# Attention's additions over key chunks moved from GpSimd to VectorE, its copies spread to ScalarE, and the conversions of a later stage spaced evenly

## The chip, the core and the metric

The kernel runs on one core of a Trainium2 chip. A core has five engines with queues of their own, each of which works through its instructions in order: TensorE (PE in the rows, its weight loads PEld), VectorE (DVE), ScalarE (ACT), GpSimd (POOL) and SyncE (SP), which here issues nearly all DMA transfers (SPq). The metric is the device time of one execution in microseconds; the program is run several times and the median counts.

## What is computed

Three steps follow on each other, all in fp32 as the reference has them:

```python
scores = scale * np.matmul(q, k.transpose(0, 1, 3, 2))      # (4, 12, 448, 64) each
scores = cap * np.tanh(scores / cap)
attn = np.exp(scores - np.max(scores, axis=-1, keepdims=True))
attn = attn / (np.sum(attn, axis=-1, keepdims=True) + 1e-09)
x = np.matmul(attn, v)                # then to 1792 tokens x 768
...
logits = x @ phi                      # soft mixture: 8 experts x 4 slots
slot_input = softmax_over_tokens(logits).T @ x
h = np.maximum(slot_input[e] @ w1[e], 0.0); slot_out[e] = h @ w2[e]
x = softmax_over_slots(logits) @ slot_out
...
h = x @ w_in; g = s * np.maximum(h, 0.0)**2 + b; out = g @ w_out
```

`w_in` and `w_out` come in 64-bit words, and have to be made fp32 on the chip before TensorE can use them.

## The kernel before

Three stages run one after the other.

**Attention with the slot inputs.** The 48 heads are handled as 24 pairs of two heads. The 448 keys of a pair lie in four chunks j: three of 128 keys for both heads (tiles of 128x896), and one of 64 keys with the two heads stacked (128x448). For each chunk TensorE makes scores (`emit_qk`, L486, tile sp), ScalarE applies tanh (L494) and exp (L508) into a tile e, and TensorE multiplies with v into one PSUM tile for the whole pair (`emit_av`, L529, and L534 for the last chunk; tile av, of which there is only one). When a pair ends, a copy takes av to xu (L410 on VectorE, L408 on ScalarE), and only then may the next pair's first L529 run. Scores are made one pair ahead of their use, from q and k that TensorE transposes (L443) and that a copy puts into qs and ks.

The denominators need the sum of e over all keys. `emit_es` (L516) adds the three large chunks of a pair elementwise into a tile es, two additions of 128x896; `emit_esl` (L521) adds the last chunk, one half-wide addition per head. TensorE then sums over partitions with a matrix of ones (`emit_den`, L552, tile dn), once for two pairs (a quad, g). Reciprocals, the logits of the mixture (lg), the transposed and normalized x (xt, xq) follow once per quad, and per six pairs (a batch) a running softmax over tokens and three slot products (sl). The last of the 24 pairs has no additions for its last two chunks: `emit_den` takes them as further terms of the matmul.

**Slots.** slp, w1 (h1p, L946) and w2 (so, L967) of the eight experts. Their weights, 25 MB for w1 and 25 MB for w2, come by DMA; ten blocks of w1 and ten of w2 are loaded while attention runs, the last six w2 blocks into the room that the conversions below leave (`cend`, which waits for the last of them). Further blocks are loaded as attention's own tiles come free at its end.

**The last two products,** PE bound, with 32 loads' worth of weights. Twenty of the 32 blocks of 64-bit words are converted while attention runs, and written to scratch memory (scr): load (`cl`, L201), two bit operations on VectorE (`conv_a`, L214 and L217), a conversion of the low words on ScalarE (`conv_f`, L224), an addition (`conv_m`, L227, VectorE or GpSimd), and the store (`cst`, L334). Two load tiles (ring w) and three result tiles exist.

**What sets the order.** Nothing in attention is ordered by hand. `ListSchedule` gets every operation with the engines that can do it and a planned duration on each (`engs`), what it needs, its priority, the ring buffers that it takes and gives back, an earliest start (`after`) and a latency until users may start (`lat`, 0.2 unless given). It plays the program through with these numbers, always placing next on the engine that can start first, and writes the instructions out in that order. Each engine then runs its list in order; a wait at the head of a list holds up all that stands behind it. Where two engines can do an operation, the planned end decides, with a surcharge where one is given: GpSimd's additions have 2.3 and 1.2, VectorE's 1.3 and 0.68 with surcharges DES and DESL, and a copy on ScalarE has the surcharge HACT. The same code with other sizes exists a second time behind a flag for inputs out of range; it doesn't run here.

Of the kernel before, what the change touches and what calls it, by code (L numbers as in the profile page):

```python
# [28 lines left out]
ACT, DVE, POOL, PE, SP = "ACT", "DVE", "POOL", "PE", "SP"  # L29


class ListSchedule:

    def __init__(self, rings):
        self.bufs = rings
        self.ops = {}

    def add(self, name, engs, fn, need=(), prio=0.0, acq=(), rel=(), after=0.0, lat=0.2):

        self.ops[name] = dict(
            engs=engs, fn=fn, need=list(need), prio=prio, acq=acq, rel=rel, after=after, lat=lat
        )

    def run(self):
        end, free, freed, holds = {}, {}, {}, {}
        got = {r: [] for r in self.bufs}
        waits, after = {}, {}  # L50
        for name, o in self.ops.items():
            need = set(o["need"])
            waits[name] = len(need)
            for d in need:
                after.setdefault(d, []).append(name)
            for x in o["rel"]:
                holds[x] = holds.get(x, 0) + 1
        ready = [name for name, n in waits.items() if n == 0]
        while ready:
            best = {}  # L60
            for name in ready:
                o = self.ops[name]
                t = max([o["after"]] + [end[d] for d in o["need"]])
                for ring, _ in o["acq"]:
                    k = len(got[ring]) - self.bufs[ring]
                    if k >= 0:
                        t = max(t, freed.get((ring, got[ring][k]), 1e9))
                if t < 1e8:
                    _, t, eng, dur = min(
                        (max(t, free.get(e, 0.0)) + d + sum(x), max(t, free.get(e, 0.0)), e, d)  # L70
                        for e, d, *x in o["engs"]
                    )
# [7 lines left out]
            end[name] = free[eng] + o["lat"]  # L80
            for ring, owner in o["acq"]:
# [14 lines left out]
def kernel(  # L96
# [16 lines left out]
    nc = tc.nc  # L113
    B, H, S, D = q.shape
# [171 lines left out]
    def run(safe):  # L286
        W1N, W2N = (4, (4,)) if safe else (10, (4, 6))
        NV, NEB, NEL, NES, NXU, NXQ, NQK = 2, 4, 2, 2, 4, 3, 2
        PX, PA, DES, DESL, HACT = -0.32, 1.5, 4.98, 1.5, 0.96
        CV0, CVP, CVA, WA = 9.33, 6.53, 20.19, 30.39  # L290

        PT, PDEN, PLG, PLW, PXT, PXM, PSO, PSL = -2.67, 1.0, 2.0, 3.4, 3.33, 2.05, 0.25, 4.75
        wctx = ExitStack()
# [76 lines left out]
        ones = c1_p.tile([128, 128], F32, name="ones")  # L370
# [22 lines left out]
        KC = S // 128  # L393
# [4 lines left out]
        spt, et, est, xut = {}, {}, {}, {}  # L398
# [4 lines left out]
        def tp(name):  # L403
            return ps_t.tile([128, 512], F32, tag="tp", name=name)
# [137 lines left out]

        def emit_den(g, _):
            pst["den", g] = ps = tp("dn")
            for j in range(4):
                n, h = 2 * g + j // 2, j % 2
                parts = [(slice(0, 128), est[n][:, h])]
                if n == NP - 1:
                    rows = slice(KL * h, KL * h + KL)
                    parts += [(slice(0, 128), et[n, KC - 1][:, h]), (rows, et[n, KC][rows, 0])]  # L550
                for i, (rows, x) in enumerate(parts):
                    nc.tensor.matmul(  # L552
                        out=ps[32 * j:32 * j + 32, 0:S], lhsT=ones[rows, 0:32], rhs=x,
                        start=(i == 0), stop=(i == len(parts) - 1),
                    )

        def emit_row_c(which, g, e):
            dnt[which, g] = t = sb_p.tile([128, S], F32, tag="dn", name="dn")
# [160 lines left out]
        ))  # L719

        def op(name, engs, f, need=(), prio=0.0, acq=(), rel=(), **kw):
            sch.add(name, engs, lambda e: f(*name[1:], e), need, prio, acq, rel, **kw)

        def cp(dve=True, hact=HACT):
            return [(DVE, 0.62)] * dve + [(ACT, 0.53, hact)]

        LAT = 2.0
        op(("const",), [(SP, 0.1)], load_const, prio=3.0, lat=LAT, after=2.0)
        for n in range(NP):
            f = 2 * n  # L730
            for w in "qk":
                i = ("ld", w, n)
# [3 lines left out]
            i = ("ld", "v", n)  # L736
# [8 lines left out]
            for j in range(KC + 1):  # L745
                u, m = f + j * 2 / (KC + 1), 1 if j < KC else 0.5
# [9 lines left out]
                rel = [(ring, (n, j))]  # L756
                if 0 < j < (KC if n < NP - 1 else KC - 1):
                    op(
                        ("es", n, j), [(POOL, 2.3), (DVE, 1.3, DES)], emit_es,
                        [("exp", n, j), ("exp", n, 0) if j == 1 else ("es", n, j - 1)], u + 1,  # L760
                        [("es", n)] if j == 1 else [], rel + [("e", (n, 0))] * (j == 1),
                    )
                if j == KC and n < NP - 1:
                    for h in range(2):
                        op(
                            ("esl", n, h), [(POOL, 1.2), (DVE, 0.68, DESL)], emit_esl, [("exp", n, j), ("es", n, j - 1)],
                            u + 1, [], rel,
                        )
                op(
                    ("av", n, j), [(PE, 0.85)], emit_av, [("exp", n, j), i] + [("av", n, j - 1)] * (j > 0), u + PA,  # L770
# [4 lines left out]
        for g in range(NQ):  # L775
            bb, gq = divmod(g, NQUAD)
            u0, last = 4 * g + 4, g == NQ - 1
# [6 lines left out]
            op(("den", g), [(PE, 0.82)], emit_den, es, u0 + PDEN, [("tp", ("den", g))], rel)  # L784
            if last:
                for j in range(2):
                    sch.add(
# [558 lines left out]
```

## Time and profile before

| what | value |
|---|---|
| times of three runs | 663.97, 662.75, 657.78 us, median 662.75 |
| the profiled execution | 664.11 us, its span 662.3 us |
| TensorE busy | 607.6 us (92%) |
| VectorE busy | 369.0 us (56%) |
| ScalarE busy | 396.5 us (60%) |
| GpSimd busy | 199.6 us (30%) |
| first scores, last product of attention with v | 9.4 us, 293.7 us |
| slots' first product (slp) | 305.9 us |
| first large product of the last stage (L1197) | 382.9 us |

The page gives each engine's busy time over the whole span, and then the span in 40 slices; the stages have different limits, so the shares of the whole say little. The rows of the next section are from the chain of work that ended last, from sums over stretches, from single instructions in order of time, and from groups by tile. In a row an idle time before an instruction stands in brackets with what ended it. The granted clock of TensorE (PEclk) is 1.00 at 2.4 GHz and 0.50 at 1.2 GHz.

### The profile page before, as it was taken

Reading aid. Unit: us, or ns where it says so; the run is one execution under the profiler, and the core shown is the slowest. Engines: PE = TensorE matmul, PEld = TensorE weight load, DVE = VectorE, ACT = ScalarE, POOL = GpSimd, SP = SyncE. Lnnn points to the kernel's source line nnn. Section 1 sums busy time; section 2 is a strip of 40 time slices with the busy share of each in tenths; the row PEclk is TensorE's granted clock in tenths of the full one; section 3 lists DMA queues with packets and bytes.
Section 4 is the critical chain, followed back from the end, with each engine's and each line's share of the span. In section 5 each row is a group of like instructions: output and inputs, shape, how many; then the busy total and the mean of one; then the engine's idle time right before and its main releaser. Section 6 shows DMA issues by size and latency. Waiting matters only on the chain.

```text
span 662.3 us, 10246 instructions
## 1 busy us (share of the span) xinstructions
PE 607.6 (92%) x3994; PEld 361.7 (55%) x3994; DVE 369.0 (56%) x518; ACT 396.5 (60%) x566; POOL 199.6 (30%) x116
## 2 busy tenths in 40 slices
PE   6979989889899999987985689999999999999995
PEld 3323333333233333333652368888888888888784
DVE  2397877768974445335460158992467669611221
ACT  4884876677666775720000188886666666656683
POOL 1694647576755555500000153421000000000000
PEclk9998989899999999996997789999999999999998
DMA  8675998979978531239999997340587779200201
GB/s 153 176 239 164 322 283 276 310 240 294 293 242 254 193 70 29 78 126 345 405 402 405 397 367 254 133 140 1 177 310 255 247 250 328 102 1 1 95 1 53
DMA packets 110345, 139.27 MB, mean 210 GB/s; under 512 B 52432, under 2 KB 84944, under 8 KB 110288
## 3 DMA queue, kind: packets, MB, share of 16 engines
q1 hardware_dynamic: 109344, 138.43, 63.6%
q8 instruction: 33, 0.54, 0.3%
q10 hardware_dynamic: 944, 0.10, 0.1%
q14 instruction: 24, 0.20, 0.1%
HBM read 125.14 MB, written 13.37 MB: 209 GB/s over the span
## 4 chain that ended last, share of the span: by engine, by line
PE 74%; DMA 12%; DVE 9%; ACT 2%; issue 1%; POOL 1%; SPq 0%; DVEq 0%; ACTq 0%; POOLq 0%
PE y L1197 23%; PE y L1198 12%; PE sp L486 10%; PE av L529 8%; DMA w2c<-in_moe_w_dram 5%; PE tr L443 3%; DMA w<-in_moe_w_out_dram 3%; PE av L534 2%; DVE cm L217 2%; PE h1p L946 2%; PE dn L552 2%; DVE cm L214 2%; PE xt L612 2%; PE gp L1129 2%; DMA w<-in_moe_w_in_dram 2%; DMA w<-scr 2%
## 5 line engine op out<-in xcount | busy, mean ns | idle before, releaser
L494 ACT ACTIVATE e<-sp,tsc 128x896 f32<-128x896 f32 x96 | 87.2, 911 | 78.9 <-PE sp L486 77.5
L1197 PE MATMUL y<-wo,gh 128*128 128x512 f32 x336 | 127.0, 400 | 0.0
L1174 DVE TENSOR_TENSOR gl<-r,gh 128x512 fp32r<-128x512 f32 (+1 forms) x65 | 44.5, 685 | 102.3 <-ACT r L1159 102.2
L486 PE MATMUL sp<-qs,ks 64*128 64x448 f32 (+1 forms) x384 | 98.4, 592 | 0.0
L1198 PE MATMUL y<-wo,gh 128*128 128x256 f32 x336 | 94.4, 281 | 0.0
L508 ACT ACTIVATE e<-e,capt 128x896 f32<-128x896 f32 x96 | 89.7, 946 | 1.8
L529 PE MATMUL av<-e,vn 128*64 128x448 f32 x288 | 74.0, 591 | 5.5 <-DVE xu L410 5.5
L516 POOL TENSOR_TENSOR es<-e 128x896 f32<-128x896 f32 x24 | 51.1, 2129 | 88.4 <-ACT e L508 55.0
L1146 ACT ACTIVATE r<-gp 128x512 f32<-128x512 f32 (+1 forms) x65 | 35.0, 539 | 60.8 <-PE gp L1129 59.3
L1197 PEld LDWEIGHTS y<-wo,gh 128*128 128x128 f32 x336 | 63.2, 188 | 13.8 <-issue 1.6
L1197 PE MATMUL y<-wo,gl 128*128 128x512 f32 x168 | 66.7, 397 | 0.0
L1198 PEld LDWEIGHTS y<-wo,gh 128*128 128x128 f32 x336 | 63.1, 188 | 1.7
L268 DVE TENSOR_REDUCE rng<-w 128x1 f32<-128x768 f32 x64 | 56.9, 944 | 0.0
L217 DVE SCALAR_TENSOR_TENSOR cm<-w,cm 128x768 int32<-128x768 int32 x32 | 53.3, 1664 | 1.1
L486 PEld LDWEIGHTS sp<-qs,ks 64*128 64x128 f32 (+1 forms) x384 | 28.1, 178 | 44.4 <-issue 24.1
L521 POOL TENSOR_TENSOR es<-es,e 64x448 f32<-64x448 f32 x35 | 49.3, 1410 | 8.4 <-ACT e L508 6.2
L516 POOL TENSOR_TENSOR es<-es,e 128x896 f32<-128x896 f32 x23 | 50.7, 2206 | 3.7 <-ACT e L508 2.7
L1159 ACT ACTIVATE r<-r,bt,st 128x512 f32<-128x512 f32 (+1 forms) x65 | 49.1, 756 | 1.8
L1159 ACT ACTIVATE gh<-r,bt,st 128x512 fp32r<-128x512 f32 (+1 forms) x65 | 49.1, 757 | 1.6
L1198 PE MATMUL y<-wo,gl 128*128 128x256 f32 x168 | 47.1, 281 | 0.0
L1197 PE MATMUL y<-woe,gh 128*128 128x512 f32 x112 | 44.3, 418 | 0.0
L214 DVE TENSOR_SCALAR cm<-w 128x768 int32<-128x768 int32 x32 | 35.4, 1107 | 15.5 <-DMA w<-in_moe_w_out_dram 8.4
(152 smaller groups left out, 907.8 us busy)
## 6 DMA issues: line engine op xcount, KB each, us to landing
w<-in_moe_w_in_dram SPq DMA_DIRECT2D x32, 768.0 KB, 5.8
w<-in_moe_w_out_dram SPq DMA_DIRECT2D x32, 768.0 KB, 6.1
w1c<-in_moe_w_dram SPq DMA_DIRECT2D x24, 1024.0 KB, 9.5
w2c<-in_moe_w_dram SPq DMA_DIRECT2D x26, 768.0 KB, 12.7
scr<-cm SPq DMA_DIRECT2D x20, 384.0 KB, 5.1
w<-scr SPq DMA_DIRECT2D x20, 384.0 KB, 5.9
qn<-in_q_dram SPq DMA_DIRECT2D x24, 224.0 KB, 4.1
kn<-in_k_dram SPq DMA_DIRECT2D x24, 192.0 KB, 4.3
```

The lines of the kernel that those rows point to most:

```text
L214: nc.vector.tensor_scalar(out=m, in0=hi, scalar1=3, scalar2=0x3FFFFFF8, op0=ALU.logical_shift_left, op1=ALU.bitwise_and)
L217: nc.vector.scalar_tensor_tensor(out=m, in0=hi, scalar=-0x40000000, in1=m, op0=ALU.bitwise_and, op1=ALU.bitwise_or)
L268: nc.vector.tensor_reduce(out=rng[:, j, i:i + 1], in_=hi, axis=AX.X, op=o, apply_absolute_value=True)
L486: nc.tensor.matmul(out=sp[:, h, 0:S] if j < KC else sp[KL * h:KL * h + KL, 0, 0:S], lhsT=ks[n][rows, 128 * j:min(128 * j + 128, S)], rhs=q ...
L494: nc.scalar.activation(out=e, in_=spt.pop((n, j))[:, 0:m, 0:S], func=AF.Tanh, scale=tsc)
L508: nc.scalar.activation(out=e, in_=e, func=AF.Exp, scale=capt)
L516: eng.tensor_tensor(out=t, in0=et[n, 0] if j == 1 else t, in1=et[n, j], op=ALU.add)
L521: eng.tensor_tensor(out=t, in0=t, in1=et[n, KC][KL * h:KL * h + KL, 0], op=ALU.add)
L529: nc.tensor.matmul(out=out, lhsT=vt[n][:, KC * h + j, :], rhs=et[n, j][:, h], start=(j == 0), stop=False)
L1159: nc.scalar.activation(out=out, in_=in_, func=AF.Identity, scale=st, bias=bt)
L1197: nc.tensor.matmul(out=ya, lhsT=lhsT, rhs=w[:, 0:512], start=first, stop=last)
L1198: nc.tensor.matmul(out=yb, lhsT=lhsT, rhs=w[:, 512:768], start=False, stop=last and i0 == per - 1)
```

## The change

It edits numbers and rules of the planner, and one loop.

- es and esl may only go to VectorE, with planned durations 1.1 and 0.63; so may the conversion's addition. In the order printed from the program, GpSimd had 47 additions of 128x896, 35 of 64x448 and 7 of the conversion in attention; VectorE had 11 and 13. Now VectorE has all 47, 46 and 20. GpSimd keeps four small additions (`lall`).
- A new rule `port` lets operations marked with it not overlap in the plan between VectorE and GpSimd.
- The surcharge of a copy on ScalarE, HACT, falls from 0.96 to 0.1. VectorE had 84 of the 96 copies and ScalarE 12; now it is 50 and 46.
- Conversions: load i may start at 20.19 + 9.5 i of the plan (CVT) rather than all from 20.19 on, with a latency of 3.0 rather than 2.0; their priority rises (CVP).
- All operations but scores, tanh and exp get a planned latency of 0.6 (LATE).
- `emit_den` of the last quad takes its further terms term by term over the four groups of 32 columns, rather than group by group.

```diff
-    def add(self, name, engs, fn, need=(), prio=0.0, acq=(), rel=(), after=0.0, lat=0.2):
+    def add(self, name, engs, fn, need=(), prio=0.0, acq=(), rel=(), after=0.0, lat=0.2, port=()):
...
+        def start(o, e, t):
+            return max(t, free.get(e, 0.0), port[0] if e in o["port"] else 0.0)
...
-        PX, PA, DES, DESL, HACT = -0.32, 1.5, 4.98, 1.5, 0.96
-        CV0, CVP, CVA, WA = 9.33, 6.53, 20.19, 30.39
+        PX, PA, HACT = -0.32, 1.5, 0.1
+        CV0, CVP, CVA, CVT, WA = 9.33, 2.0, 20.19, 9.5, 30.39
+        LATE = 0.6
...
-                parts = [(slice(0, 128), est[n][:, h])]
+                parts.append([(slice(0, 128), est[n][:, h])])
...
-                for i, (rows, x) in enumerate(parts):
-                    nc.tensor.matmul(
...
+            for i in range(3):
+                for j in range(4):
+                    if i < len(parts[j]):
+                        rows, x = parts[j][i]
+                        nc.tensor.matmul(
...
+            kw = {"lat": LATE if name[0] not in ("qk", "tanh", "exp") else 0.2, **kw}
...
-                        ("es", n, j), [(POOL, 2.3), (DVE, 1.3, DES)], emit_es,
+                        ("es", n, j), [(DVE, 1.1)], emit_es,
...
-                            ("esl", n, h), [(POOL, 1.2), (DVE, 0.68, DESL)], emit_esl, [("exp", n, j), ("es", n, j - 1)],
+                            ("esl", n, h), [(DVE, 0.63)], emit_esl, [("exp", n, j), ("es", n, j - 1)],
...
-            op(("cl", i), [(SP, 2.19)], cv_load, [], pr - 6, [("w", i)], lat=LAT, after=CVA)
-            op(("ca", i), [(DVE, 2.0)], cv_a, [("cl", i)], pr, [("cm", i), ("ce", i)], [("w", i)])
+            op(("cl", i), [(SP, 2.19)], cv_load, [], pr - 6, [("w", i)], lat=3.0, after=CVA + CVT * i)
+            op(("ca", i), [(DVE, 1.55)], cv_a, [("cl", i)], pr, [("cm", i), ("ce", i)], [("w", i)], port=BOTH)
...
-            op(("cmul", i), [(DVE, 1.23), (POOL, 1.83)], cv_m, [("cf", i)], pr, [], [("ce", i)])
+            op(("cmul", i), [(DVE, 0.95)], cv_m, [("cf", i)], pr, [], [("ce", i)], port=BOTH)
```

The lines of the changed kernel stand 7 to 14 higher (L410 is L418, L521 is L529, L552 is L564). Three places show what the new numbers do to the order.

VectorE early in attention, at the end of the third pair, before: the third conversion (w_437) stands ahead of the copy of that pair (xu).

```order
L521 TENSOR_TENSOR es<-es,e 64x448
L214 TENSOR_SCALAR cm<-w_437 128x768
L217 SCALAR_TENSOR_TENSOR cm<-w_437,cm 128x768
L410 COPY xu<-av 128x448
L410 COPY qs<-tr 128x448
L410 COPY ks<-tr 128x448
L588 TENSOR_TENSOR lw<-rowt,rd 112x512
```

The same place now, from the copy xu of that pair on; the first conversion's addition is the row ahead of it.

```order
L234 ISA cm<-cm,ce 128x1536
L418 COPY xu<-av 128x448
L600 TENSOR_TENSOR lw<-rowt,rd 112x512
L524 TENSOR_TENSOR es<-e 128x896
L609 TENSOR_REDUCE lall<-lw 112x128
L524 TENSOR_TENSOR es<-es,e 128x896
L629 TENSOR_TENSOR xq<-xt,rd 112x4x128
L529 TENSOR_TENSOR es<-es,e 64x448 x2
L629 TENSOR_TENSOR xq<-xt,rd 112x4x128
L221 TENSOR_SCALAR cm<-w_432 128x768
L224 SCALAR_TENSOR_TENSOR cm<-w_432,cm 128x768
```

The additions of a pair now stand between the other work of VectorE, and the second conversion comes a whole pair's work after the copy.

TensorE at the last quad before: the sums dn of the last two pairs, between the last pair's products with v.

```order
L529 MATMUL av<-e,vn 64x448 x2
L552 MATMUL dn<-es,ones 32x448 x3
L552 MATMUL dn<-e,ones 32x448 x2
L552 MATMUL dn<-es,ones 32x448
L552 MATMUL dn<-e,ones 32x448 x2
L529 MATMUL av<-e,vn 64x448 x2
L565 MATMUL rowt<-ident,dn 112x128 x4
L534 MATMUL av<-e,vn 64x448 x2
```

And now:

```order
L537 MATMUL av<-e,vn 64x448 x2
L564 MATMUL dn<-es,ones 32x448 x4
L564 MATMUL dn<-e,ones 32x448 x4
L537 MATMUL av<-e,vn 64x448 x2
L542 MATMUL av<-e,vn 64x448 x2
L577 MATMUL rowt<-ident,dn 112x128 x4
```

The four sums over es now come first and together, and the pair's last products stand ahead of the transposes rowt.

SyncE's queue behind the last conversion before: the store scr_117 is the last of the conversions, and the loads of v for eight more pairs follow.

```order
L362 DMA w2c<-in_moe_w_dram 128x2x768 x2
L334 DMA scr_117<-cm 128x768
L362 DMA w2c<-in_moe_w_dram 128x2x768
L429 DMA vn<-in_v_dram 128x2x192
L434 DMA vn<-in_v_dram 64x64 x2
L419 DMA qn<-in_q_dram 112x8x64
L424 DMA kn<-in_k_dram 128x6x64
L425 DMA kn<-in_k_dram 64x2x64
L362 DMA w2c<-in_moe_w_dram 128x2x768 x3
```

And now; the six w2c behind scr_117 are those that wait for `cend`.

```order
L208 DMA w_2208<-in_moe_w_out_dram 128x1536
L342 DMA scr_115<-cm 128x768
L437 DMA vn<-in_v_dram 128x2x192
L442 DMA vn<-in_v_dram 64x64 x2
L342 DMA scr_116<-cm 128x768
L437 DMA vn<-in_v_dram 128x2x192
L442 DMA vn<-in_v_dram 64x64 x2
L342 DMA scr_117<-cm 128x768
L370 DMA w2c<-in_moe_w_dram 128x2x768 x6
L364 DMA w1c<-in_moe_w_dram 128x2x1024 x2
L370 DMA w2c<-in_moe_w_dram 128x2x768 x3
```

The last store now stands behind the last load of attention (vn of the last pair), and the six blocks of w2 behind it.

## Rows read from the trace of the kernel before

**Rows 1.** Chain that ended last, attention: start us, us, what.

```profile
30.16 0.90 PE av L534 x4
...
196.41 0.90 PE av L534 x4
...
238.05 0.90 PE av L534 x4
...
261.31 0.90 PE av L534 x4
...
292.75 0.95 PE av L534 x4
```

**Rows 2.** Sums over two stretches of attention: busy us (instructions) of each engine.

```profile
core 0: us, PE busy (x) PEld busy (x) DVE busy (x) ACT busy (x) POOL busy (x), PEclk, DMA share, GB/s
31.00:197.30 166.30, 150.74 (x771) 53.73 (x770) 132.62 (x159) 115.02 (x140) 108.45 (x59) 0.94 0.87 266
197.30:239.00 41.70, 41.70 (x219) 15.07 (x218) 19.36 (x34) 28.99 (x32) 21.68 (x13) 1.00 0.66 202
```

**Rows 3.** Instructions in order of time, between the third and the fourth pair.

```profile
40.70 5.20 DVE L214 TENSOR_SCALAR cm<-w 128x768 int32<-128x768 int32 x1
...
43.42 2.07 POOL L516 TENSOR_TENSOR es<-e 128x896 f32<-128x896 f32 x1
...
48.58 0.61 DVE L410 COPY xu<-av 128x448 f32<-128x448 f32 x1
...
49.24 3.25 PE L529 MATMUL av<-e,vn 128*64 128x448 f32 x8 [4.57 <-DVE xu L410]
```

**Rows 4.** Tile cm, attention: duration ns min/median/max; idle before it until what.

```profile
L214 DVE TENSOR_SCALAR cm<-w x20: 550/972/5204, 31.8 to 181.2; 128x768 int32<-128x768 int32 x20
L217 DVE SCALAR_TENSOR_TENSOR cm<-w,cm x20: 958/1778/2736, 32.4 to 182.4; 128x768 int32<-128x768 int32 x20
...
L227 DVE CUSTOM_DVE_ANT_0 cm<-cm,ce x13: 941/959/2604, 50.8 to 192.7; 128x1536 uint16<-128x1536 uint16 x13
...
  DMA w<-in_moe_w_out_dram: 8.4, 4
  DMA w<-in_moe_w_in_dram: 6.9, 4
```

**Rows 5.** Tile es, attention: duration ns min/median/max.

```profile
L516 POOL TENSOR_TENSOR es<-es,e x23: 2077/2097/2823, 18.0 to 274.1; 128x896 f32<-128x896 f32 x23
L521 DVE TENSOR_TENSOR es<-es,e x11: 622/622/1231, 20.1 to 266.2; 64x448 f32<-64x448 f32 x11
```

**Rows 6.** Costs by line and form, attention: count, busy us, mean ns.

```profile
L603 DVE TENSOR_TENSOR lw<-lall,lr 112x512 f32<-112x512 f32 x4 | 2.8, 692 | 0.1
...
L224 ACT ACTIVATE ce<-w 128x768 int32<-128x768 uint32 x20 | 18.1, 907 | 1.6 <-DMA w<-in_moe_w_in_dram 1.6
...
L408 ACT COPY xu<-av 128x448 f32<-128x448 f32 x3 | 1.6, 533 | 2.2 <-PE av L534 2.2
```

**Rows 7.** The chain again, the end of attention.

```profile
270.90 0.89 PE dn L552 x8
...
286.27 4.99 PE dn L552 x16
```

**Rows 8.** Instructions in order of time, ScalarE and SyncE, end of attention.

```profile
213.32 1.57 SPq L362 DMA_DIRECT2D w2c<-in_moe_w_dram  x3
271.14 0.99 ACT L494 ACTIVATE e<-sp,tsc 128x896 f32<-128x896 f32 x1
...
274.33 9.38 SPq L356 DMA_DIRECT2D w1c<-in_moe_w_dram  x2
...
293.82 1.39 SPq L362 DMA_DIRECT2D w2c<-in_moe_w_dram  x3
```

**Rows 9.** Sums over 5 us at the start of the slots, columns as in rows 2.

```profile
300.00:305.00 5.00, 3.07 (x28) 1.44 (x28) 3.24 (x11) 0.91 (x3) 0.53 (x1) 0.54 1.03 408
```

**Rows 10.** The chain, end of the slots.

```profile
333.31 32.91 DMA w2c<-in_moe_w_dram x2
```

**Rows 11.** DMA issues by line: count, KB each, median us to landing.

```profile
scr<-cm SPq DMA_DIRECT2D x20, 384.0 KB, 5.1
```

More of the change, by code (lines that the diff above doesn't have):

```diff
@@ L39, in __init__ @@
         self.ops = {}
-    def add(self, name, engs, fn, need=(), prio=0.0, acq=(), rel=(), after=0.0, lat=0.2):
+    def add(self, name, engs, fn, need=(), prio=0.0, acq=(), rel=(), after=0.0, lat=0.2, port=()):
         self.ops[name] = dict(
-            engs=engs, fn=fn, need=list(need), prio=prio, acq=acq, rel=rel, after=after, lat=lat
+            engs=engs, fn=fn, need=list(need), prio=prio, acq=acq, rel=rel, after=after, lat=lat, port=port
         )
@@ L48, in run @@
         end, free, freed, holds = {}, {}, {}, {}
+        port = [0.0]
         got = {r: [] for r in self.bufs}
@@ L69, in run @@
                     _, t, eng, dur = min(
-                        (max(t, free.get(e, 0.0)) + d + sum(x), max(t, free.get(e, 0.0)), e, d)
-                        for e, d, *x in o["engs"]
+                        (start(o, e, t) + d + sum(x), start(o, e, t), e, d) for e, d, *x in o["engs"]
                     )
@@ L80, in run @@
             end[name] = free[eng] + o["lat"]
+            if eng in o["port"]:
+                port[0] = free[eng]
             for ring, owner in o["acq"]:
@@ L544, in emit_den @@
             pst["den", g] = ps = tp("dn")
+            parts = []
             for j in range(4):
                 n, h = 2 * g + j // 2, j % 2
-                parts = [(slice(0, 128), est[n][:, h])]
+                parts.append([(slice(0, 128), est[n][:, h])])
                 if n == NP - 1:
                     rows = slice(KL * h, KL * h + KL)
-                    parts += [(slice(0, 128), et[n, KC - 1][:, h]), (rows, et[n, KC][rows, 0])]
-                for i, (rows, x) in enumerate(parts):
-                    nc.tensor.matmul(
-                        out=ps[32 * j:32 * j + 32, 0:S], lhsT=ones[rows, 0:32], rhs=x,
-                        start=(i == 0), stop=(i == len(parts) - 1),
-                    )
+                    parts[j] += [(slice(0, 128), et[n, KC - 1][:, h]), (rows, et[n, KC][rows, 0])]
+            for i in range(3):
[3 more added lines that the diff above has]
+                        nc.tensor.matmul(
+                            out=ps[32 * j:32 * j + 32, 0:S], lhsT=ones[rows, 0:32], rhs=x,
+                            start=(i == 0), stop=(i == len(parts[j]) - 1),
+                        )
         def emit_row_c(which, g, e):
@@ L727, in run @@
         LAT = 2.0
+        BOTH = (DVE, POOL)
         op(("const",), [(SP, 0.1)], load_const, prio=3.0, lat=LAT, after=2.0)
@@ L758, in run @@
                     op(
-                        ("es", n, j), [(POOL, 2.3), (DVE, 1.3, DES)], emit_es,
+                        ("es", n, j), [(DVE, 1.1)], emit_es,
                         [("exp", n, j), ("exp", n, 0) if j == 1 else ("es", n, j - 1)], u + 1,
-                        [("es", n)] if j == 1 else [], rel + [("e", (n, 0))] * (j == 1),
+                        [("es", n)] if j == 1 else [], rel + [("e", (n, 0))] * (j == 1), port=BOTH,
                     )
@@ L765, in run @@
                         op(
-                            ("esl", n, h), [(POOL, 1.2), (DVE, 0.68, DESL)], emit_esl, [("exp", n, j), ("es", n, j - 1)],
-                            u + 1, [], rel,
+                            ("esl", n, h), [(DVE, 0.63)], emit_esl, [("exp", n, j), ("es", n, j - 1)],
+                            u + 1, [], rel, port=BOTH,
                         )
@@ L783, in run @@
                 rel += [("e", (NP - 1, KC - 1)), ("el", (NP - 1, KC))]
-            op(("den", g), [(PE, 0.82)], emit_den, es, u0 + PDEN, [("tp", ("den", g))], rel)
+            op(("den", g), [(PE, 2.4 if last else 0.82)], emit_den, es, u0 + PDEN + last, [("tp", ("den", g))], rel)
             if last:
```

## Prediction

> **What bounds the kernel now.** I first cut the run into stages by the chain of work that ended last. In the last stage TensorE is the chain almost alone, and the change touches nothing there. In the slots the chain goes through loads of weights [rows 10], and the DMA engines are full at about 405 GB/s [rows 9]: their length is given by bytes, not by when attention ends. What is left is attention, and here the chain gives the last product of each pair [rows 1]. Pair 15 ends at 196.41 + 0.90 = 197.31, pair 19 at 238.95: 10.41 us per pair. Pair 2 ends at 31.06, so the 13 pairs before 197.31 took 166.25 us, or 12.79 each. The pairs 20 and 21, which hold a batch's softmax and slot products, took 262.21 - 238.95 = 23.26 us, that is 2.4 us more than two plain ones.
>
> The sums over these two stretches [rows 2] say why. In the later one TensorE is busy all 41.70 us at a granted clock of 1.00. In the earlier one it is idle for 166.30 - 150.74 = 15.6 us and its clock is 0.94 in the mean. At full clock the 13 pairs and two batches want 13 x 10.41 + 2 x 2.4 = 140.2 us; 166.2 - 140.2 = **26.0 us are lost there**, 15.6 idle and the remaining 10.4 at the lower clock level, which the trace grants in stretches around such idle times. VectorE and GpSimd are not full either (80% and 65%). The loss comes from order and long single instructions: L214 takes 5.20 us while GpSimd works through three instructions, the copy xu behind it starts at 48.58, and TensorE's next product has waited 4.57 us for it [rows 3]. L214 has a minimum of 0.55 us and a median of 0.97, L217 0.96 and 1.78 [rows 4]. In the stretch without conversions nothing of this is left.
>
> **The change, part by part.** *The conversions on VectorE.* With GpSimd silent but for four small additions, I take the shortest times: 0.55 + 0.96 + 0.95 = 2.5 us for the three instructions of one [rows 4]. Twenty conversions now lie over about 20 pairs, 2.5 us per pair.
>
> *The additions on VectorE.* The half-wide one has been seen there, 0.62 us [rows 5]. The wide one (896 elements) has not. Between 448 elements in 0.622 and 512 in 0.692 [rows 6] lie 1.09 ns per element, so 0.622 + 448 x 0.00109 = 1.1 us; it can't be under the half-wide 0.62, and two half-wide ones are 1.24. I take 1.1, since 512 elements are measured. That is 47 x 1.1 + (46 - 11) x 0.62 = 73 us more, 3.1 per pair. On GpSimd one took 2.1.
>
> *Copies to ScalarE.* 34 leave VectorE at 0.61 each [rows 3], 0.9 us per pair, and cost ScalarE 0.53 each [rows 6], 0.75 per pair.
>
> *What each engine then has to do per pair.* The stretch without conversions gives VectorE 19.36 / 4 = 4.8 us and ScalarE 28.99 / 4 = 7.2 [rows 2]. VectorE: 4.8 + 3.1 - 0.9 + 2.5 = 9.5. ScalarE: 7.2 + 0.75 + 0.91 for the low words [rows 6] = 8.9. TensorE: 10.41 + 2.4 / 6 = 10.8. TensorE stays the longest; VectorE gets to 88% of it. With 1.24 for the wide addition VectorE has 9.8, which changes nothing.
>
> Here the Trainium skill speaks against the change: Perfetto Trace Analysis, Optimizing Scalar/DVE Operations, says that work may be given away to ScalarE or even GpSimd when VectorE is saturated, and this change takes work from GpSimd onto VectorE. The same passage warns that the two share a read port, so that moving work between them might not help. By the first half VectorE's load would decide; the rows put it at 9.5 of 10.8.
>
> *What stays lost.* If the 15.6 us idle and the 10.4 at the low clock all went, 26.0 us would be won; that is the bound above, seen in the stretch without conversions. The bound below is nothing. What remains is the wait at the head of VectorE's queue for a conversion's load: 8 waits, 15.3 us [rows 4]. Behind it stand copies and additions that TensorE waits for. The loads are now asked for more evenly and with 1 us more allowance, and the copy xu often goes to ScalarE; but VectorE has only 1.3 us of slack per pair to catch up. I let 6 us of such waits reach TensorE, about two fifths, and add the clock in the proportion seen, 10.4 to 15.6: **10 us stay, 16 are won**.
>
> *The last dn.* Eight instructions of a plain dn take 0.89 us, since four groups of 32 columns run beside each other; the last one takes 4.99 for sixteen [rows 7]. Taken term by term it has three rounds of at most 0.89, or 2.7: 2.3 us less, in TensorE's queue at the end of attention, where nothing hides it. At worst, if the rounds don't overlap, nothing is won.
>
> *Loads at the end of attention.* The last conversion moves. Before, the six w2c blocks behind it were issued by 214.9, and DMA was nearly idle until the first block that waits for the last pair's end, at 293.82 [rows 8]. Now the last low-word conversion on ScalarE stands right behind the third tanh of the second-last pair, which before was at 271.14 [rows 8]. Then 0.99 for the tanh, 0.91 and 0.95 for conversion and addition, some 0.2 between: 274.2 on the old clock, 293.7 - 274.2 = 19.5 us ahead of attention's last product, 17.2 with the shorter dn. Six blocks of 0.79 MB and the two of w1 (1.05 MB) are 6.8 MB, 17 us at 408 GB/s [rows 9]. So they end just when attention does; if the blocks have to wait for the store's landing (5.1 us [rows 11]), 5 us later, and what follows is a stream that is bound by bytes. I take **2.5 us** given back, between 0 and 5. Were the conversions 10 us later, 10 more would be lost.
>
> *Cost at nothing:* the new latency and the port rule only move operations in the plan; storing and loading scr is the same bytes at other times, hidden as long as DMA has room in attention (its share was 0.87 in the earlier stretch).
>
> **Sum** against the profiled execution: 664.1 - 16 - 2.3 + 2.5 = 648.3. It is 1.4 above the median of the runs shown (662.75), so I forecast 647 for the median.
>
> **Rivals.** *All of it* (0.12): no more than 3 us stay lost and the loads cost nothing, as between 197 and 239 us. 664.1 - 26 - 2.3 + (0 to 3) - 1.4 = 634 to 638. Against it: that stretch had VectorE at 46%, not 88%.
>
> *Half or nothing* (0.20): the waits for conversion loads reach TensorE in full. 15.3 us with the clock's share (x 1.67) are 25.6, and 2.5 for the loads: 664.1 - 26 - 2.3 + 25.6 + 2.5 - 1.4 = 662.5; with 18 us lost instead of 10 it is 655. To this belongs the case that the change doesn't do what it says, because the long L214 and L217 have another cause than GpSimd: then a conversion stays at its measured 1.2 + 1.8 + 1.0, VectorE at 9.5 - 2.5 + 4.0 = 11.0 us per pair is just above TensorE's 10.8, and no slack is left to catch up with. For it speaks only that DMA is busy at the same times; against it the minima, and the row of 5.20 us, which ends when GpSimd's third instruction has ended.
>
> *Slower* (0.10): VectorE becomes the bound. Its pair of 9.5 us is above the old pace of 12.79 once every conversion waits over 3.3 us for its load at the queue's head, behind which now all additions stand as well. The mean over the 8 waits was 1.9. At 4 us on each of 20: 20 x (13.5 - 12.79) = 14, so 664.1 + 14 - 2.3 + 2.5 - 1.4 = 677.
>
> **How the numbers follow.** My forecast, 10 us lost of 26 and 2.5 given back, with its bounds (3 to 18 us lost, 0 to 5 given back), is 638 to 655 and has 0.58. The range of 8 in 10 leaves out the best case and most of the slower one: 638 to 661. A measurement of this kernel tells about 1% from no change: faster by more is under 656.1, which the forecast, the first rival and a small part of the second fill: 0.72. Within 1%: 0.18. Slower: 0.10.
>
> **What would show it.** L221 and L224 (the two bit operations) at medians near 0.56 and 0.96, with no value over 2; the wide addition at 1.1. VectorE at about 9.5 us per pair and TensorE at 11.2 in the stretch of conversions, with idle time under 8 us up to the last conversion and fewer stretches at 1.2 GHz. Attention's last product near 278, the last dn under 3 us. The w2c blocks behind `cend` issued some 17 us ahead of it, and the first of the three w2c that wait for the last pair without a gap in DMA behind them. I'm wrong if TensorE still waits for copies that stand behind conversions waiting for their loads, or if the slots take longer by more than 5 us.

## The result, and the profile after

The changed kernel takes 638.45 us in the median of 5 runs (637.11 to 643.45) where the kernel before takes 661.15 (657.78 to 663.97): a ratio of 0.9665, 95% interval 0.9627 to 0.9704, so 3.3% faster. I had forecast 647 with a range of 638 to 661: the direction held, the range only just (two of the five runs lie under 638), and the gain was half as large again as forecast. The profiled execution took 643.45 us (span 641.6) and is the slowest of the five, 5 us longer than the median; the sums below are made against it.

The chain of work that ended last, through attention (start us, us, what); it answers to [rows 1] and [rows 7]:

```profile
32.65 0.90 PE av L542 x4
...
179.17 0.90 PE av L542 x4
...
221.08 0.90 PE av L542 x4
...
269.43 2.51 PE dn L564 x16
271.94 0.90 PE av L537 x4
272.84 0.95 PE av L542 x4
...
286.06 0.91 PE slp L948 x8
...
313.43 32.55 DMA w2c<-in_moe_w_dram x2
```

Pair 2 ends at 33.55, pair 15 at 180.07, pair 19 at 221.98 and the last at 273.79. Against the trace of before that is, by stretch: +2.5 us up to pair 2, -19.7 in the 13 pairs up to pair 15 (146.5 for 166.2), +0.3 in the next four, -2.9 in the last five with the shorter dn, -0.4 in the slots (the load that ends them is in at 313.43 + 32.55 = 345.98 where it was in at 366.24), -0.4 behind them. Together -20.6, which is 664.11 - 643.45.

The same two stretches as in [rows 2], cut at the pairs' new ends, columns as there, and the stretch from 160 us to the end of attention:

```profile
33.50:180.10 146.60, 142.78 (x767) 51.72 (x766) 114.09 (x174) 116.22 (x150) 3.07 (x2) 0.98 0.86 256
180.10:222.00 41.90, 41.90 (x221) 15.49 (x222) 33.67 (x49) 35.13 (x46) 0.00 (x0) 1.00 0.62 175
160.00:273.70 113.70, 113.70 (x627) 40.22 (x623) 89.52 (x139) 88.72 (x115) 2.47 (x2) 1.00 0.59 185
```

TensorE is idle for 3.8 us of the first stretch where it was idle for 15.6, and its granted clock is 0.98 in the mean where it was 0.94. The conversion's tile cm and the sums es, with duration in ns as min/median/max, and what ended the idle time before cm:

```profile
L221 DVE TENSOR_SCALAR cm<-w x20: 497/559/570, 34.3 to 252.0; 128x768 int32<-128x768 int32 x20
L224 DVE SCALAR_TENSOR_TENSOR cm<-w,cm x20: 957/960/961, 34.9 to 252.6; 128x768 int32<-128x768 int32 x20
L234 DVE CUSTOM_DVE_ANT_0 cm<-cm,ce x20: 947/953/959, 41.7 to 256.8; 128x1536 uint16<-128x1536 uint16 x20
...
  DMA w<-in_moe_w_in_dram: 15.0, 5
...
L524 DVE TENSOR_TENSOR es<-e x24: 1081/1083/1093, 19.6 to 263.8; 128x896 f32<-128x896 f32 x24
```

The long instructions of [rows 4] are gone, and the wide addition, never seen on VectorE before, takes 1.083 us. The waits for a conversion's load at the head of VectorE's queue are still there, 15.0 us in 5. One of them reaches TensorE with more than a microsecond; in order of time, with idle time and what ended it in brackets:

```profile
139.30 0.39 SPq L208 DMA_DIRECT2D w<-in_moe_w_in_dram  x1
...
145.92 0.56 DVE L221 TENSOR_SCALAR cm<-w 128x768 int32<-128x768 int32 x1 [5.44 <-DMA w<-in_moe_w_in_dram]
...
147.39 0.62 DVE L418 COPY dn<-dn 128x448 f32<-128x448 f32 x1
...
148.15 1.07 PE L577 MATMUL rowt<-ident,dn 128*112 128x128 f32 x4 [3.14 <-DVE dn L418]
```

The load is issued at 139.30, the conversion waits 5.44 us for it, the copy dn stands behind the conversion, and TensorE waits 3.14 us for the copy. From 148 to 160 us the granted clock is 0.72 in the mean (it was 1.00 in the 28 us ahead).

The plan spaces the conversions evenly; the trace does so only up to that wait. Up to 146 us they start at least 7.9 us after each other, and from 166 us on in four twos, 2.2 to 3.3 us apart. The first of the twos:

```profile
165.92 0.56 DVE L221 TENSOR_SCALAR cm<-w 128x768 int32<-128x768 int32 x1
168.12 0.55 DVE L221 TENSOR_SCALAR cm<-w 128x768 int32<-128x768 int32 x1
```

With GpSimd silent the twos cost nothing: TensorE is busy all 113.7 us from 160 us on.

On SyncE's queue the last conversion's store, and behind it the blocks that wait for `cend`:

```profile
257.73 0.50 SPq L342 DMA_DIRECT2D scr<-cm  x1
258.28 4.92 SPq L370 DMA_DIRECT2D w2c<-in_moe_w_dram  x6
263.24 3.62 SPq L364 DMA_DIRECT2D w1c<-in_moe_w_dram  x2
273.84 1.40 SPq L370 DMA_DIRECT2D w2c<-in_moe_w_dram  x3
```

### The profile page after: what moved, and what is told of

It reads as the page before. It is cut to its first block, busy times and chain, and to the rows that moved or that the text cites. A ratio compares the mean times of both kernels' runs of the same rounds, so it can differ in the third digit from the quotient of the medians.

```text
span 641.6 us, 10167 instructions
## 1 busy us (share of the span) xinstructions
PE 601.2 (94%) x3994; PEld 362.1 (56%) x3994; DVE 383.9 (60%) x573; ACT 409.1 (64%) x600; POOL 37.4 (6%) x27
## 4 chain that ended last, share of the span: by engine, by line
PE 83%; DMA 10%; DVE 3%; ACT 1%; SPq 1%; issue 1%; DVEq 0%; ACTq 0%
PE y L1211 25%; PE sp L494 13%; PE y L1212 12%; PE av L537 9%; DMA w2c<-in_moe_w_dram 5%; PE tr L451 4%; PE av L542 3%; PE h1p L960 2%; PE gp L1143 2%; PE rowt L577 2%; PE xt L624 2%; DMA w<-in_moe_w_in_dram 2%; DMA w<-scr 2%; PE dn L564 2%; PE lg L592 1%; PE so L981 1%
## 5 line engine op out<-in xcount | busy, mean ns | idle before, releaser
L1188 DVE TENSOR_TENSOR gl<-r,gh 128x512 fp32r<-128x512 f32 (+1 forms) x65 | 42.3, 652 | 103.8 <-ACT r L1173 103.7
L537 PE MATMUL av<-e,vn 128*64 128x448 f32 x288 | 71.9, 574 | 0.0
L1211 PE MATMUL y<-woe,gh 128*128 128x512 f32 x112 | 45.6, 427 | 0.0
L1098 ACT CAST woe<-w 128x768 fp32r<-128x768 f32 x2 | 1.7, 830 | 66.3 <-DMA w<-scr 66.3
L537 PEld LDWEIGHTS av<-e,vn 128*64 128x64 f32 x288 | 15.2, 137 | 41.7 <-issue 28.4
L1167 ACT ACTIVATE r<-r 128x512 f32<-128x512 f32 (+1 forms) x65 | 37.1, 573 | 1.7
L224 DVE SCALAR_TENSOR_TENSOR cm<-w,cm 128x768 int32<-128x768 int32 x32 | 36.9, 1154 | 1.1
L1211 PEld LDWEIGHTS y<-wo,gl 128*128 128x128 f32 x168 | 31.6, 188 | 7.4
```

Source lines behind the costliest of these rows:

```text
L224: nc.vector.scalar_tensor_tensor(out=m, in0=hi, scalar=-0x40000000, in1=m, op0=ALU.bitwise_and, op1=ALU.bitwise_or)
L537: nc.tensor.matmul(out=out, lhsT=vt[n][:, KC * h + j, :], rhs=et[n, j][:, h], start=(j == 0), stop=False)
L1167: nc.scalar.activation(out=t, in_=t, func=AF.Square)
L1188: eng.tensor_tensor(out=gl, in0=t, in1=f32(gh), op=ALU.subtract)
L1211: nc.tensor.matmul(out=ya, lhsT=lhsT, rhs=w[:, 0:512], start=first, stop=last)
```

## The experiments

Two theories stood at first. **S** (T1 in the expectations), the prediction's: GpSimd's additions hold VectorE's instructions up, and with GpSimd silent this ends. **O** (T2): the order (spacing of the conversions, slack) takes the hold-ups off TensorE's path. After the first four kernels a third came in, **C**: copies on ScalarE give VectorE the room for its conversions. Every run stands in the table, with three moments of its trace: **A**, when attention's last product ends; **C**, when the last group of the six w2c blocks that wait for the conversions is issued; **E**, when the load that ends the slots is in. **N** counts the conversions that start less than 5 us after the one before (of 19).

| kernel | median us | ratio to before (95%) | A | C | E | N |
|---|---|---|---|---|---|---|
| before | 661 to 663 | 1 | 293.7 | 213 | 366.2 | 5 |
| before + additions on VectorE | 662.1 | 1.001 (0.999 to 1.003) | 268.1 | 277.9 | 364.8 | 3 |
| before + slack | 657.4 | 0.996 (0.992 to 0.999) | 286.0 | 215 | 358.4 | 4 |
| before + copies | 654.5 | 0.987 (0.979 to 0.995) | 286.6 | 226 | 358.5 | 4 |
| before + spacing | 643.0 | 0.973 (0.969 to 0.977) | 273.6 | 254 | 346.2 | 0 |
| before + additions + copies | 644.7 | 0.976 (0.971 to 0.981) | 271.6 | 230 | 345.2 | 5 |
| changed, GpSimd adds again | 641.2 | 0.968 (0.964 to 0.972) | 271.3 | 255 | 344.0 | 0 |
| changed, no spacing | 642.7 | 0.970 (0.967 to 0.974) | 273.7 | 234 | 346.4 | 5 |
| changed, copies as before | 641.4 | 0.970 (0.965 to 0.976) | 267.1 | 257.3 | 344.3 | 4 |
| changed, no slack | 637.3 | 0.964 (0.960 to 0.969) | 267.5 | 250 | 340.6 | 0 |
| the same, five rounds | 636.7 | 0.963 (0.961 to 0.966) | 267.3 | 250 | 339.8 | 0 |
| changed, five rounds | 640.0 | 0.968 (0.964 to 0.971) | 274.1 | 258.6 | 346.8 | 4 |
| changed + work on GpSimd | 653.3 | 0.987 (0.983 to 0.991) | 284.3 | 269.9 | 357.7 | 4 |

### Additions alone, on the kernel before

```diff
-                        ("es", n, j), [(POOL, 2.3), (DVE, 1.3, DES)], emit_es,
+                        ("es", n, j), [(DVE, 1.1)], emit_es,
```

and likewise esl (0.63), the conversion's addition (0.95) and its bit operations (1.55).

> The kernel before with one part of the change: the additions over chunks of keys and the conversion's second step on VectorE alone, none on GpSimd; conversions not spaced, the former copies, slack and order of the last row sums. The theory of a silent GpSimd (T1): VectorE's conversion instructions have medians near 0.56 and 0.96 us and none over 2 us, product 15 of attention ends near 184 where it ended at 197 before, and the time is 642 to 648 us, most of the 22.7 us. The rival, that the spacing and the slack of the order bring the gain (T2): 655 to 661 us, with TensorE still idle over 10 us up to product 15, because VectorE has more work in the same bunched order.

Both theories missed the time or its reason. Attention did what S says: its last product ends 25.5 us earlier (268.1, where it was 293.7), L214 and L217 have medians of 0.560 and 0.959, and TensorE is busy without a break from 31 to 200 us. And yet the time is that of before. SyncE's queue, then the chain at the end of the slots:

```profile
268.54 9.26 SPq L334 DMA_DIRECT2D scr<-cm  x3
277.85 4.94 SPq L362 DMA_DIRECT2D w2c<-in_moe_w_dram  x6
282.83 1.01 SPq L356 DMA_DIRECT2D w1c<-in_moe_w_dram  x2
...
316.80 48.02 DMA w2c<-in_moe_w_dram x3
364.84 11.75 DMA w<-scr
```

The conversions run on to the end of attention, the last stores leave at 268.54 and later, and the six w2c blocks behind them at 277.85, **after** attention's last product. From there the DMA engines are full (403 GB/s from 280 to 340), and the slots end where they ended before. The gain was not missing; it was given back to loads that had become late. VectorE was busy 216 of the 255 us from 20 to 275, which left it little room to do the conversions sooner.

### The additions back on GpSimd, in the changed kernel

```diff
-                        ("es", n, j), [(DVE, 1.1)], emit_es,
+                        ("es", n, j), [(POOL, 2.3), (DVE, 1.3, DES)], emit_es,
```

likewise esl and the conversion, and no `port` rule.

> The changed kernel with the additions and the conversion's second step allowed on GpSimd again as before; spacing, slack, copies and the new order of the last row sums stay. T1: GpSimd and VectorE hold each other up again, conversion instructions of 2.5 to 5 us are back, and the time is 652 to 660 us (only the 2.5 us of the last row sums and a few us of order kept). T2: 639 to 644 us.

641.2 us: O's answer, and S's is wrong by over 10 us. The hold-ups are back (L224 at a median of 1.775 us and up to 2.791), and GpSimd is busy 149 us of the 255 from 20 to 275, but TensorE is busy 252.2 of them at a clock of 1.00. Here the conversions start 7.7 to 12.6 us after each other.

### The conversions not spaced, in the changed kernel

```diff
-                pr - 6, [("w", i)], lat=3.0, after=CVA + CVT * i)
+                pr - 6, [("w", i)], lat=LAT, after=CVA)
```

and CVP back at 6.53.

> The changed kernel with the conversions asked for as before (no distance of 9.5 us between them, priority step 6.53, 2.0 us for a load); all else as changed. T1: 638 to 642 us, since VectorE has room for a conversion in any pair (9.5 of 10.8 us). T2: 648 us or more, with TensorE idle over 8 us in pairs that hold two conversions.

642.7 us: 0.7 above S's answer, far from O's. The conversions now start 1.5 to 19.7 us after each other, in twos from the first on, and it matters little as long as GpSimd is silent. The step is smaller than planned, since the changed kernel has twos as well (2.2 to 20.0 us); the plain case follows below. So neither edit is necessary while the other is there.

### Work on GpSimd that nobody waits for

```diff
...
+            else:
+                nc.gpsimd.tensor_tensor(out=nz, in0=nz, in1=nz, op=ALU.mult)
...
```

> The changed kernel with work added on GpSimd alone: after each quad of heads 12 multiplications of 128 x 512 floats on a tile of their own, which nobody reads or waits for (some 14 us in each 22). VectorE's and ScalarE's instructions and their order stay. If GpSimd holds VectorE up merely by being at work (T1): conversion instructions over 2 us are back on VectorE, and the time is 643 to 655 us. If what hurt before was that results of GpSimd came late (2.1 us instead of 1.1) and not a hold-up: VectorE's durations stay at 0.56 and 0.96 us and the time is 637 to 640 us.

653.3 us: here the hold-up is isolated, and it is real. Groups of instructions from 20 to 275 us (busy us, mean ns | idle before), first in the changed kernel:

```profile
L529 DVE TENSOR_TENSOR es<-es,e 64x448 f32<-64x448 f32 x46 | 28.0, 608 | 1.6 <-ACT e L516 1.0
L224 DVE SCALAR_TENSOR_TENSOR cm<-w,cm 128x768 int32<-128x768 int32 x20 | 19.2, 959 | 0.7
...
L418 DVE COPY xu<-av 128x448 f32<-128x448 f32 x14 | 8.7, 622 | 7.2 <-PE av L542 7.1
...
L612 DVE TENSOR_REDUCE lr<-lw 112x128 f32<-112x512 f32 x7 | 7.3, 1046 | 0.0
```

and with the work on GpSimd:

```profile
L532 DVE TENSOR_TENSOR es<-es,e 64x448 f32<-64x448 f32 x46 | 50.8, 1104 | 1.6 <-ACT e L519 1.0
L224 DVE SCALAR_TENSOR_TENSOR cm<-w,cm 128x768 int32<-128x768 int32 x20 | 30.1, 1507 | 0.7
...
L421 DVE COPY xu<-av 128x448 f32<-128x448 f32 x14 | 8.6, 614 | 4.4 <-PE av L545 4.4
L621 DVE TENSOR_REDUCE lr<-lw 112x128 f32<-112x512 f32 x6 | 6.2, 1036 | 0.0
...
L595 POOL TENSOR_TENSOR nz<-nz 128x512 f32<-128x512 f32 x119 | 170.7, 1435 | 8.2
```

VectorE's instructions are the same, in number and in size, and its busy time goes from 193.79 to 242.43 us. What grows are the instructions that read two tiles of SBUF (es 608 to 1104 ns), and the bit operations on words from SBUF. Copies out of PSUM (xu) and reductions (lr) stay. The Trainium skill, SBUF — State Buffer, Who interferes with whom, says that a VectorE instruction with two inputs in SBUF contends with a GpSimd instruction that reads SBUF, and that a `tensor_reduce` does not; these rows agree. The wide additions, with two inputs in SBUF as well, grow by 3 to 15% only. A moves by 10.5 us and C by 11.6: hold-ups cost time when VectorE already has 194 of 255 us to do. But this is another loss than that of the kernel before: TensorE's waits are 16 of at most 1.1 us each, from a VectorE that is nearly full, where in the kernel before the few waits were of up to 4.6.

### Additions and copies, on the kernel before

```diff
-        PX, PA, DES, DESL, HACT = -0.32, 1.5, 4.98, 1.5, 0.96
+        PX, PA, DES, DESL, HACT = -0.32, 1.5, 4.98, 1.5, 0.1
```

on top of the additions.

> The kernel before with two parts of the change: all additions on VectorE, and copies on ScalarE wherever that is free (0.1 for 0.96). The additions alone ended attention 25 us earlier, but VectorE was so full that its conversions ran on to the end of attention, the weight loads that wait for them came after it, and nothing was left. Theory C (copies give VectorE the room): conversions end before 215, and the time is 640 to 646 us. Theory O (spacing and slack of the order are needed for that): 655 us or more, with conversions past 240.

644.7 us, C's answer: the copies bring VectorE from 216 to 193 us of 255, the last store leaves at 214.62, and the gain of the additions is kept. This kernel is also the plain case of silence without spacing: its conversions start 2.0 to 17.1 us after each other, five of them less than 5 us after the last.

### The copies as before, in the changed kernel

```diff
-        PX, PA, HACT = -0.32, 1.5, 0.1
+        PX, PA, HACT = -0.32, 1.5, 0.96
```

> The changed kernel with the copies shared as before (0.96 for 0.1); additions on VectorE, spacing, slack and the new order of the last row sums stay. Theory C: VectorE is full again (over 210 us of 255), conversions run past 240, and the time is 652 to 662 us, though attention ends early. Theory O: the spacing keeps the conversions in their pairs and the time is 638 to 644 us.

641.4 us, nearer to O's answer, but C's mechanism is in the trace: VectorE has 215 us of 255 to do. The conversions don't stay spaced (1.7 to 20.9 us apart), but they end sooner than with the additions alone, where VectorE was as full: C comes at 257.25 instead of 277.85. The higher priority may be why; it was not tried alone. Even 257.25 is just too late: attention ends earliest of all, at 267.1, yet the load that ends the slots is in at 344.34, as 257.25 + 87 has it.

### The slack taken out of the changed kernel

```diff
-        LATE = 0.6
+        LATE = 0.2
```

> The changed kernel without the slack of 0.6 us that the order leaves between an operation and the one that needs it (0.2 as before); all else as changed. If VectorE with its additions and without hold-ups is enough (theories C and S): 637 to 643 us. If the slack is what keeps TensorE from waiting (theory O): 646 us or more, with TensorE waits over 10 us between 20 and 280 (3.8 us in the changed kernel).

637.3 us: the slack is not what keeps TensorE going. It seemed to cost time, so both kernels were run once more, side by side:

> The changed kernel itself, to stand beside the one without the slack on one chip: 637 to 641 us; attention's slots + 60 us and the conversions' end + 87 us come within 1 us of each other.

> The changed kernel without the slack of 0.6 us (0.2 as before), once more. If the slack lengthens attention, as its first profile says (last product 267.5 where the changed kernel has 273.7, conversions' end 244 where it has 258): 635 to 638 us, 1 to 3 us below the changed kernel. If that was the profiled execution's luck: within 1 us of it.

636.73 us (635.75 to 637.67) without the slack, 639.99 (637.82 to 643.9) with it: the two just don't overlap, and the medians are 3.3 us apart. The traces are further apart, since the one with the slack is of its slowest execution and the other of its fastest. This is the fastest kernel of the study. In its trace TensorE is busy for all 142.24 us of the 13 pairs from 30.99 to 173.23, at a granted clock of 1.00, and its conversions are spaced to the end (5.6 to 14.8 us apart). What the slack loses starts at the very beginning. The changed kernel, in this second trace:

```profile
8.12 1.53 ACTq L719 DMA_DIRECT2D phibd<-in_moe_phi_dram  x2
...
8.81 0.62 SPq L427 DMA_DIRECT2D qn<-in_q_dram  x1
...
11.66 0.67 SPq L725 DMA_DIRECT2D st<-in_moe_s_dram  x1
...
12.90 0.63 SPq L432 DMA_DIRECT2D kn<-in_k_dram  x1
...
13.29 0.58 PE L451 MATMUL tr<-ident,qn 112*128 112x112 f32 x4 [1.26 <-DMA qn<-in_q_dram]
...
14.70 0.99 PE L451 MATMUL tr<-ident,kn 128*128 128x128 f32 x4 [0.83 <-DMA kn<-in_k_dram]
```

and without the slack:

```profile
11.13 1.43 ACTq L719 DMA_DIRECT2D phibd<-in_moe_phi_dram  x2
11.70 0.64 SPq L432 DMA_DIRECT2D kn<-in_k_dram  x1
12.50 0.63 PE L451 MATMUL tr<-ident,qn 112*128 112x112 f32 x4
...
13.48 0.72 PE L451 MATMUL tr<-ident,kn 128*128 128x128 f32 x4 [0.36 <-DMA kn<-in_k_dram]
```

The slack moves ScalarE's issue of the phi loads ahead of its first tanh, to 8.1 instead of 11.1, in front of the q and k that TensorE needs next; those are in later, and from 12 to 24 us the granted clock is 0.86 instead of 1.00. In all seven traces with the slack the phi loads are issued at 8.1 to 8.3 and the first pair ends at 25.3 to 26.8; in all seven without it, the kernel before among them, at 11.0 to 11.2 and at 23.1 to 23.3. That phi delays q is argued from this order, and was not tried alone. The slack also puts the loads of s and b (L725) ahead of the next k, which is issued at 12.90 instead of 11.70; which of the two costs the 2.5 us is open.

### The parts that move the order, each alone on the kernel before

The copies alone (the HACT line above):

> The kernel before with one part of the change: copies on ScalarE wherever that is free; additions stay on GpSimd, nothing spaced, no slack. VectorE's hold-ups of 2 to 5 us stay. If the hold-ups cost time only because copies that TensorE waits for stand behind them on VectorE (theory C): 641 to 648 us. If the slack or the spacing takes them off the path (theory O): 655 to 663 us.

654.5 us, between the two: A comes 7.1 us earlier.

The slack alone (0.6 for 0.2 in all but scores, tanh and exp):

> The kernel before with one part of the change: the slack of 0.6 us in the order. Additions on GpSimd, copies shared as before, conversions not spaced. VectorE's hold-ups stay. By the two bounds read so far, the slots end at the later of the attention's slots + 60 us and the end of the conversions + 87 us; the second has room here, so the time follows attention. If slack takes the hold-ups off the path: last product before 280, 646 to 652 us. If it does not: 657 to 664 us.

657.4 us, at the edge of "does not": by the ratio 3 us faster, with an interval from 0.5 to 5.5 (the profiled execution, 2.5 us below its median, has A 7.6 us earlier). The slack helps a little at most, and its first pair ends 2.4 us later than before.

The spacing alone:

```diff
-        CV0, CVP, CVA, WA = 9.33, 6.53, 20.19, 30.39
+        CV0, CVP, CVA, WA = 9.33, 2.0, 20.19, 30.39
...
-                pr - 6, [("w", i)], lat=LAT, after=CVA)
+                pr - 6, [("w", i)], lat=3.0, after=CVA + 9.5 * i)
```

> The kernel before with one part of the change: conversions 9.5 us apart with 3.0 us for a load. Additions on GpSimd, copies shared as before, no slack. If conversions in bunches are what brings the hold-ups on the path: last product of attention before 282, 648 to 655 us. If a single conversion beside GpSimd is enough for that: 656 to 664 us.

643.0 us, better than the better of the two answers: a ratio of 0.973, where the whole change, run beside it, has 0.968. Three numbers bring most of the gain, with the additions shared between GpSimd and VectorE as before. Its tile cm in attention, and its sums from 20 to 275 us:

```profile
L214 DVE TENSOR_SCALAR cm<-w x20: 550/1478/2351, 33.3 to 236.9; 128x768 int32<-128x768 int32 x20
L217 DVE SCALAR_TENSOR_TENSOR cm<-w,cm x20: 957/1775/2786, 35.2 to 237.5; 128x768 int32<-128x768 int32 x20
...
20.00:275.00 255.00, 250.64 (x1328) 88.46 (x1327) 172.39 (x236) 190.29 (x229) 152.81 (x88) 1.00 0.74 227
```

and the same sums of the kernel before:

```profile
20.00:275.00 255.00, 239.44 (x1246) 85.27 (x1244) 173.16 (x228) 179.25 (x213) 157.33 (x88) 0.96 0.72 218
```

VectorE and GpSimd are as busy as before, and the two bit operations are held up longer than in [rows 4] in the median (only the longest, 5.20 us, has no match). But TensorE's busy time goes from 239.4 to 250.6 us, and its clock from 0.96 to 1.00; between 31 and 200 us it waits for VectorE 1.8 us in two waits, where it was 15.5 us in seven. What differs in the trace is the distance: the conversions start 7.6 to 13.9 us after each other, where in the kernel before it was 2.8 to 14.3, five of the 19 distances under 5.

### What the runs say together

Two conditions had to meet for the 26 us of the kernel before: conversions bunched on VectorE, **and** hold-ups by GpSimd under them. Without the bunches (spacing alone, A 20.1 us earlier) or without the hold-ups (additions and copies, bunched as before, 22.0 earlier; additions alone 25.5) attention is as short as with the whole change (19.9). Waits for a conversion's load at VectorE's head don't sort the kernels: they are 15.3 us in the kernel before, 10.2 with the spacing alone, and 20.1 in the changed kernel without spacing. Then a second bound shows. In the 14 traces (the table's 13 and that of the section on the result), E is within 1.1 us of the later of A + 72.5 and C + 87.5 (where C lies before 240, the first alone). Both numbers are read from these same traces; the second decides in three of them, by 25 us with the additions alone, 5 with the copies as before and 0.6 with work on GpSimd. The two numbers differ by 15 us, about the time that the six w2c and two w1c blocks between them take (17 us by the prediction's working). The changed kernel stands at the corner: 273.8 + 72.5 = 346.3 and 258.3 + 87.5 = 345.8, measured 346.0. There a shorter attention alone brings nothing more, as in the kernel with its copies as before; only without the slack do both move, by 6.8 and 8.7 us between the two traces.

## Why the prediction was right, and where not

**The bound now.** Right: the time followed attention's end, and the slots kept their length (366.24 - 293.70 = 72.5 us before, 72.2 after).

**The costs.** Right: 0.56, 0.96 and 0.95 us for a conversion, 1.083 for the wide addition (1.1 taken), 2.51 for the last dn (2.7). VectorE's pair came to 114.09 / 13 = 8.8 us (9.5 taken). TensorE's came to 11.3, near the 11.2 that I had named; but by my own sum, with 10 us lost, it had to be (140.2 + 10) / 13 = 11.6.

**Why the time falls.** Half right. The long L214 and L217 do come from GpSimd, which the kernel with added work shows, and with GpSimd silent the time falls without any spacing (644.7, with the copies moved as well so that the loads are not late). But silence was not needed: the time falls nearly as far with the long instructions kept (643.0, and 641.2 with the rest of the change). The change holds two cures for one loss, and the prediction counted one of them. The step "the loss comes from order and long single instructions" had both words in it, and I then priced only the second. [Rows 3] could have been read the other way: the copy xu started late because a whole conversion had been planned ahead of it, and the order printed above shows that too.

**What stays lost.** Mis-sized: 10 us taken, 146.5 - 140.2 = 6.3 measured. The waits for loads at VectorE's head stayed (15.0 us of 15.3), but only one of them reached TensorE with more than a microsecond: 3.1 us, and a low clock behind it. That is the case that I had named as a sign of being wrong; it came once, with 3.1 us where 6 were taken. Without the slack the 13 pairs take 142.2 with TensorE busy throughout at full clock, so the 140.2 was 2 us too low as a bound.

**The loads at the end of attention.** The place was right (C 15.5 us ahead of the last product, 17 to 19 taken), the price not: 2.5 us taken, nothing measured, since at that distance the two bounds are equal. "Were the conversions 10 us later, 10 more would be lost" was right: the kernel with the additions alone has them 20 us later and loses 19.

**Not in the prediction.** The slack was costed at nothing: the new latency and the port rule "only move operations in the plan". It moved the phi loads ahead of q, and all seven traces with it are 2 us or more late by the first pair.

**The sum.** -16 - 2.3 + 2.5 = -15.8 was forecast against the profiled execution, and -20.6 came. The difference is 3.7 more in the pairs with conversions, 2.9 at the loads, 0.6 at dn and 0.4 behind the slots, less 2.5 lost at the start and 0.3 in pairs 16 to 19. The rest of the 8.6 us between 647 and the median is the profiled execution of the changed kernel, 5.0 us above that median, where I had allowed 1.4. The median lies inside the range by half a microsecond, and that much is luck.

**The rivals.** "Half or nothing" wanted all 15.3 us of waits for loads to reach TensorE, which waited 3.8 in all. "Doesn't do what it says" fell with the medians of L221 and L224. "Slower" fell too: VectorE waited 15 us at its head, far from 3.3 for each of 20. "All of it", 634 to 638, is what the kernel without the slack reaches, at 636.7; that is another kernel, and doesn't make the rival right.

What stays open: the spacing was three numbers (distance, latency, priority), and they were not tried apart, so that it is the distance which cures is argued from the traces.

## What to carry to other kernels

When a change removes a cause and the time falls, put the cause back with the rest of the change in place: here the time stayed down, because two conditions had to meet and either cure was enough. Read the order and the trace again each time: here the planner spaced the conversions evenly with the additions on GpSimd, and only in part without them. A gain in one stage counts only until the next stream is late, so write down both moments that release the transfers behind it, and look which of them decides. Slack in a planner's numbers is an edit to the order, the loads at the start included, and wants its own row in the trace.

## What the runs showed of the hardware

- With GpSimd at work on SBUF (119 multiplications of 128x512, 1.44 us each), VectorE's half-wide addition of two SBUF tiles took 1.10 us instead of 0.61 and the bit operation L224 1.51 instead of 0.96, while copies out of PSUM stayed at 0.61 to 0.62 and reductions at 1.04 to 1.05. The wide addition grew less, from 1.09 to 1.25 in the first and from 1.08 to 1.12 in the second of a pair; why is open.
- Sixteen products for four groups of 32 columns took 4.99 us group by group [rows 7] and 2.51 term by term, with the same instructions.
- A wait of TensorE of 3.14 us was followed by 12 us at a mean granted clock of 0.72, that is a stretch of them at the level of 1.2 GHz, so that the wait cost about 5 us in all (pair 13 took 16.2 us, and 11.4 without the slack).
